# Retention and a routed layer of experts on one core: the decay spread by a matmul, sends ahead of expert 0's cut, 224 columns in expert 0's halves

## The chip, the core and the metric

One core of a Trainium2 chip runs the whole program. The time is the device time of one execution in microseconds (us), the median of the runs shown. Engines: TensorE (PE; its weight loads are PEld), VectorE (DVE), ScalarE (ACT), GpSimd (POOL) and SyncE (SP), which issues most DMAs. Each engine works through its instructions in the order of the program; the order is written out by hand.

## What is computed

q, k and v are (4, 8, 768, 64): batch, heads, positions, head size. A linear attention with a decay per head gives x, 3072 tokens of 512 features, and each token goes through the one expert of eight that its gate chooses:

```python
state = gamma[None, :, None, None] * state + np.einsum('bhd,bhe->bhde', k[:, :, t], v[:, :, t])
y[:, :, t] = scale * np.einsum('bhd,bhde->bhe', q[:, :, t], state)
...
logits = x @ w_gate
expert_idx = np.argmax(logits, axis=1)
...
h = np.maximum(xe @ w1[e], 0.0)
ye = h @ w2[e]
out[mask] = gate_w[mask, None] * ye
```

w1 is (8, 512, 1024), w2 is (8, 1024, 512), all in float32.

## The kernel before

The 3072 tokens are 24 chunks of 128, six to a batch. A loop (L442) takes them in 12 pairs, a = 2k and b = 2k+1. In a pair `scores` multiplies k and q (TensorE) and VectorE multiplies the result by the masks M (L242), `carry` and `output` add the state's part and the chunk's part into Y, `turn_out` multiplies Y by the decay G into xT (VectorE, L288), and `update` adds the chunk into the state, from `vs`, which is v scaled by GpSimd in `scale` (L228). `gate_rows` belongs to the pair before: `logits`, then `rows` (transposes on TensorE into `xp`, copied by ScalarE into the ring `xn`), then `finish_logits`.

When a group of six, four or two chunks has its logits, `gating` chooses the expert (`choose`), takes the exponential (`soft`), counts places with small products (`rank`, `slots`, `advance`) and computes the weights. `send_x` then has GpSimd scatter the 128 rows of a chunk into a table in DRAM, `xs_dram`, by expert (indirect DMA, L629): 24 sends, spread over the pairs by the table SENDS. FETCHES and SPLITS say in which pair expert 0's weights are loaded and split into a high and a low part (L135 on ScalarE, L136 on VectorE or GpSimd). These products take three terms: high by high, high by low and low by high.

Expert 0 is done in two halves of up to EARLY = 256 tokens: those of the first two batches while the attention still runs, the others behind it. After pair 9, `load_x` (L170) and `load_meta` read the first half's rows back from DRAM. In the last pair VectorE turns them (`turn_slices`, L639), ScalarE casts the high part and GpSimd subtracts for the low part (`cut_slices`, L648 and L649, tile xhl). `hidden` (L671) and `result` (L688) are expert 0's two layers for this half; `fill(n)` puts n half steps of `hidden` between the last steps of the gate. The second half (`xg1`, `xhl1`) and the experts 1 to 7 follow in `moe_main` (L818, L843, L845).

The loads of q, k and v go into a ring of five buffers, so load(2k+5) waits until pair k has used its own. SP issues all of them, the weights, `load_x` and the zeroing of rows behind a region, in the order of the program. GpSimd takes its `scale`, its splits, the sends and the low parts in the order of the program too.

Of the kernel before, what the change touches and what calls it, by code (L numbers as in the profile page):

```python
# [20 lines left out]
P = 128  # L21
# [6 lines left out]
CAPS = [256, 452, 424, 412, 400, 392, 376, 360]  # L28
EARLY = 256
# [28 lines left out]
for _name, _w in (("causal", 128), ("cv", 6 * H), ("ratio", 6 * (H // 2)), ("ident", 128), ("iota", 128),  # L58
                  ("desc", 16), ("tok", NTOK), ("blk", 24), ("ebase", E9),
                  ("rev", E1), ("eid", E1), ("caps", E1), ("row", 4), ("slot", JMAX), ("place", 4)):  # L60
    OFF[_name] = (_n, _n + _w)
    _n += _w
# [4 lines left out]
def _constants():  # L67
# [3 lines left out]
    def put(name, v):  # L71
# [6 lines left out]
    put("iota", np.broadcast_to(p[None, :].astype(np.float64), (P, P)))  # L78
# [16 lines left out]
    g = np.repeat(turned[:, :, None] ** (np.arange(C) + 1.0)[None, None, :] / np.sqrt(np.float64(D)), D, axis=0)  # L95
    u = (p[:, None] < p[None, :]).astype(np.float64)
    return (c.astype(np.float32), np.ascontiguousarray(g.astype(np.float32)),
            u.astype(np.float32))
# [3 lines left out]
def retention_moe(ctx, tc, qkv, wg, wts, cst, gdec, ustr, out):  # L102
# [86 lines left out]
    with ExitStack() as actx:  # L189
# [138 lines left out]
        def gating(k):  # L328
# [29 lines left out]
            def rank():  # L358
                pf = v["pf"] = ps_s.tile([P, NB, E9], F32, name="pf", tag="sp")
# [47 lines left out]
        us32 = rawp.tile([P, P], F32, name="us32", tag="raw")  # L407
# [17 lines left out]
        nc.sync.dma_start(out=us32, in_=ustr)  # L425
# [10 lines left out]
        def gate_rows(k):  # L436
            logits(k - 1)
            rows(2 * k - 2)
            rows(2 * k - 1)
            finish_logits(k - 1)  # L440

        for k in range(NCH // 2):  # L442
# [13 lines left out]
            carry(b, c == 0)  # L456
            sends = list(range(*SENDS.get(k, (0, 0))))
# [24 lines left out]
            output(a)  # L482
# [3 lines left out]
            if not last:  # L486
                update(b + 1)
            if k == 1:
                nc.vector.tensor_copy(out=us, in_=us32)
                nc.vector.tensor_scalar(out=run, in0=k_("ebase"), scalar1=1.0 / P, scalar2=None, op0=ALU.mult)  # L490
                nc.vector.tensor_copy(out=wgs[:, :, E:E + 1], in_=wgs[:, :, 0:1])
                gate_rows(k)
            for g in range(2 * k + AHEAD, min(2 * k + AHEAD + 2, NCH)):
                load(g, slice(0, 4 if g % CPB < CPB - 1 else 3))
            if k == 1:
                for e in (0, E):
                    clear(slice(e * N + FILLED, e * N + FILLED + ZROWS))
            if k == 9:
# [4 lines left out]
            if k in FETCHES:  # L503
                fetch(0, FETCHES[k])

        stages["rank"]()
        for name in ("slots", "advance", "weights"):
            stages[name]()
        for g in range(SENDS[NCH // 2 - 1][1], GROUPS[-2][0]):
            send_x(g)  # L510
# [3 lines left out]
        rows(NCH - 1)  # L514
        for g in range(GROUPS[-2][0], GROUPS[-1][0]):
            send_x(g)
        fill(FILL[1])
        finish_logits(NCH // 2 - 1)
        final = gating(len(GROUPS) - 1)
        final["choose"]()  # L520
        final["soft"]()
        for i in (12, 13):
            split(0, *divmod(i, 4), nc.vector, 1)
        fill(FILL[2])
        lows(2, nc.gpsimd)
        final["rank"]()
        final["slots"]()
        final["weights"]()
        for i in (14, 15):
            split(0, *divmod(i, 4), nc.vector, 1)  # L530
        for g in range(GROUPS[-1][0], NCH):
            send_x(g)
# [13 lines left out]
        with nc.allow_low_precision(reason="one nonzero term, a small integer"):  # L546
            nc.vector.tensor_reduce(out=eid7, in_=se, axis=AX.X, op=ALU.add)

# [38 lines left out]
        pieces = ((0, P), (4, P // 2), (6, P // 2))  # L587
# [69 lines left out]
def early_half(tc, yo, rx, wp, ps, wparts, xhl, sidx0, meta0, out):  # L657
# [6 lines left out]
    def hidden(f, part=None):  # L664
# [16 lines left out]
    def result(j, part):  # L681
        if part == 0:
            pys[j] = ps.tile([P, DM], F32, name="py0", tag="sp")
        py = pys[j]
        for f in range(4 * part, 4 * part + 4):
            whi, wlo = wparts[0, 2 + f // 4]
            for i, (a, h) in enumerate(((whi, hh), (wlo, hh), (whi, hl))):
                nc.tensor.matmul(out=py, lhsT=h[:, f, j * P:(j + 1) * P], rhs=a[:, f % 4, :],  # L688
# [3 lines left out]
        nc.vector.tensor_scalar(out=sliced(yo[:, j, :]), in0=featured(py), scalar1=meta0[:, j, 1:2], scalar2=None,  # L692
                                op0=ALU.mult)

    def send(j):
        scatter_rows(tc, out, sidx0[:, j:j + 1], yo[:, j, :])
# [5 lines left out]
def moe_main(ctx, tc, wparts, fetch, split, xhl1, xgs, clear_behind, load_x, load_meta, token_index, regions, beyond, limit, natural,  # L702
# [14 lines left out]
    pys = [ps_y.tile([P, DM], F32, name=f"py{i}") for i in range(2)]  # L717
    out_slices = out.rearrange("n (q m) -> (n q) m", q=4)
# [56 lines left out]
    with tc.manual_schedule():  # L775
        for e in range(E):
# [222 lines left out]
```

## Time and profile before

| | |
|---|---|
| median of 3 runs | 404.08 us (403.95 to 404.31) |
| the profiled execution | 404.0 us |
| its span, first to last instruction | 402.2 us |
| TensorE busy | 388.8 us, 97% |
| VectorE, ScalarE, GpSimd busy | 249.9, 154.0, 165.8 us |
| DMA | 80.55 MB, mean 200 GB/s |

Times in the views are microseconds from the first instruction. The timeline gives for each group of neighbouring instructions its start, its length, engine, line, operation, result and operands, and in brackets the idle time of the engine before it with what ended the idle time. Neighbouring products overlap, so a group's length is not the sum of its products. The attention takes the first 100 us, expert 0's first half about 100 to 125, its second half 125 to 148, the other experts the rest.

### The profile page before, as it was taken

How to read it: one execution, taken by the hardware profiler on the slowest of the kernel's cores; microseconds unless marked ns; L12 is line 12 of the kernel's file. 1: busy time of each engine (PE TensorE's matmuls, PEld its weight loads, DVE VectorE, ACT ScalarE, POOL GpSimd, SP SyncE). 2: the span in 40 equal slices, each digit the busy share in tenths (PEclk: the TensorE clock that was granted, in tenths of full speed). 3: DMA queues.
4: the chain of work that ended last, by engine and by line, in shares of the span. 5: the costliest groups of instructions: out<-in, count | busy, mean ns of one | idle time of the engine just before them, and what ended most of it. 6: DMA issues, size and time to landing. Idle time of an engine off the chain costs nothing. (4 is left out here: it accounts for less than half of the span.)

```text
span 402.2 us, 8329 instructions
## 1 busy us (share of the span) xinstructions
PE 388.8 (97%) x3276; PEld 359.4 (89%) x3276; DVE 249.9 (62%) x467; ACT 154.0 (38%) x307; POOL 165.8 (41%) x152
## 2 busy tenths in 40 slices
PE   8889999998999999999999999999999999999994
PEld 4778888896989979999999999999999999999972
DVE  4448757786685577672866387467738657675410
ACT  2236345463623444431543245145324515523200
POOL 0334536854771032000386057118605822850741
PEclk9999999999999999999999999999999999999999
DMA  7998799982547959365348347915654783530111
GB/s 278 404 417 304 264 406 424 404 363 76 213 135 208 255 175 285 115 175 143 123 146 228 115 137 235 233 51 210 203 145 130 246 216 107 165 128 2 53 47 48
DMA packets 30745, 80.55 MB, mean 200 GB/s; under 512 B 5130, under 2 KB 19342, under 8 KB 24176
## 3 DMA queue, kind: packets, MB, share of 16 engines
q1 hardware_dynamic: 25664, 67.31, 51.6%
q0 software_dynamic: 5040, 12.69, 8.4%
q8 instruction: 26, 0.43, 0.4%
q14 instruction: 15, 0.12, 0.1%
HBM read 65.50 MB, written 15.22 MB: 201 GB/s over the span
## 5 line engine op out<-in xcount | busy, mean ns | idle before, releaser
L629 POOL DMA_INDIRECT out<-Z,sidx x80 | 94.0, 1176 | 136.9 <-DVE Z L770 115.6
L136 DVE TENSOR_TENSOR wlo<-raw,whi 128x1024 fp32r<-128x1024 f32 (+1 forms) x66 | 79.1, 1200 | 16.6 <-ACT whi L135 16.2
L135 ACT CAST whi<-raw 128x1024 fp32r<-128x1024 f32 (+1 forms) x72 | 67.4, 951 | 5.0 <-DMA raw<-w 5.0
L823 ACT ACTIVATE hh<-ph 128x256 fp32r<-128x256 f32 (+7 forms) x64 | 31.5, 492 | 93.1 <-PE ph L818 92.8
L845 PE MATMUL py<-hh,whi 128*128 128x452 f32 (+5 forms) x192 | 66.9, 349 | 0.0
L845 PE MATMUL py<-hl,whi 128*128 128x452 f32 (+5 forms) x192 | 66.8, 348 | 0.0
L845 PE MATMUL py<-hh,wlo 128*128 128x452 f32 (+5 forms) x192 | 66.8, 348 | 0.0
L824 DVE SCALAR_TENSOR_TENSOR hl<-ph,hh 128x256 fp32r<-128x256 f32 (+7 forms) x64 | 35.5, 555 | 34.4 <-ACT hh L823 33.7
L818 PE MATMUL ph<-xh,whi 128*128 128x452 f32 (+6 forms) x224 | 50.1, 345 | 0.5 <-ACT xh L648 0.5
L818 PE MATMUL ph<-xl,whi 128*128 128x452 f32 (+6 forms) x224 | 50.2, 345 | 0.0
L818 PE MATMUL ph<-xh,wlo 128*128 128x452 f32 (+6 forms) x224 | 50.0, 345 | 0.0
L818 PEld LDWEIGHTS ph<-xh,whi 128*128 128x128 f32 x224 | 40.6, 188 | 1.6 <-ACT xh L648 0.9
L818 PEld LDWEIGHTS ph<-xl,whi 128*128 128x128 f32 x224 | 40.8, 188 | 0.7
L818 PEld LDWEIGHTS ph<-xh,wlo 128*128 128x128 f32 x224 | 40.7, 188 | 0.7
L648 ACT CAST xh<-xt 128x512 fp32r<-128x512 f32 (+7 forms) x26 | 14.3, 554 | 60.8 <-DVE xt L639 60.8
L845 PEld LDWEIGHTS py<-hl,whi 128*128 128x128 f32 x192 | 36.0, 188 | 0.8
L845 PEld LDWEIGHTS py<-hh,whi 128*128 128x128 f32 x192 | 36.1, 188 | 0.7
L845 PEld LDWEIGHTS py<-hh,wlo 128*128 128x128 f32 x192 | 36.1, 188 | 0.7
L228 POOL TENSOR_TENSOR vs<-qkv_t,cs 128x512 f32<-128x512 f32 x19 | 20.1, 1059 | 35.5 <-DMA qkv_t<-qkv 32.9
L242 DVE TENSOR_TENSOR Sb<-sp,xgs 128x512 f32<-128x512 f32 x48 | 29.9, 682 | 4.9 <-PE sp L239 4.9
L765 DVE STREAM_TRANSPOSE Z<-py 128x416 f32<-128x416 f32 (+3 forms) x24 | 15.0, 627 | 27.3 <-PE py L845 27.2
L629 POOL DMA_INDIRECT xs_dram<-xn,KEY x24 | 24.6, 1026 | 17.4 <-DVE xt L639 7.7
(130 smaller groups left out, 528.8 us busy)
## 6 DMA issues: line engine op xcount, KB each, us to landing
raw<-w SPq DMA_DIRECT2D x32, 1024.0 KB, 5.6
qkv_t<-qkv SPq DMA_DIRECT2D x19, 1024.0 KB, 9.6
qkv_t<-qkv SPq DMA_DIRECT2D x4, 768.0 KB, 7.7
xgs<-xs_dram SPq DMA_DIRECT2D x12, 211.2 KB, 4.7
xgs<-xs_dram SPq DMA_DIRECT2D x8, 195.0 KB, 4.0
out<-Z,sidx POOLq DMA_INDIRECT x80, 4.0
xs_dram<-zero SPq DMA_DIRECT2D x6, 195.0 KB, 5.7
qkv_t<-qkv SPq DMA_DIRECT2D x2, 512.0 KB, 7.0
```

Of the source, the lines that this page charges most:

```text
L135: nc.scalar.copy(out=hi[:, h], in_=raw[:, h])
L136: engine.tensor_tensor(out=lo[:, h], in0=raw[:, h], in1=hi[:, h].bitcast(F32), op=ALU.subtract)
L228: engine.tensor_tensor(out=vs, in0=qs[g][:, 2].rearrange("a (h d) -> a h d", d=D), in1=cv[:, c, :].unsqueeze(2).broadcast_to([P, H, D]), o ...
L242: nc.vector.tensor_tensor(out=Sb[:, r], in0=sps[r], in1=M[:, r], op=ALU.mult)
L629: sc = tc.nc.gpsimd.indirect_dma_start(out=out, out_offset=bass.IndirectOffsetOnAxis(ap=index, axis=0), in_=rows, in_offset=None, bounds_c ...
L648: nc.scalar.copy(out=xh[:, :, sl], in_=src)
L765: nc.vector.transpose(out=Zs[e][:, 0:nb, k, :], in_=py[:, 0:32 * nb].rearrange("p (j c) -> p j c", c=32))
L818: nc.tensor.matmul(out=ph[:, :cap], lhsT=wparts[e, f // 4][a][:, kd, fo:fo + P], rhs=x[:, kd, :cap], start=(n == 0), stop=(n == 3 * KD - 1))
L823: nc.scalar.activation(out=hh[:, :cap], in_=ph[:, :cap], func=AF.Relu)
L824: nc.vector.scalar_tensor_tensor(out=hl[:, :cap], in0=ph[:, :cap], scalar=0.0, in1=hh[:, :cap].bitcast(F32), op0=ALU.max, op1=ALU.subtract)
L845: nc.tensor.matmul(out=py[:, :cap], lhsT=a[:, f % 4, k * P:(k + 1) * P], rhs=x[:, :cap], **se)
```

## The change

- G is no longer loaded (256 KB). A table of 2 x 640 numbers is, ahead of the first q, k and v; one product spreads it over 128 partitions into PSUM and ScalarE copies it to G. Four of 13 warm products go. The strictly lower triangle `us` is computed from two tables instead of loaded, and `iota` has 8 columns instead of 128. Chunks 0 and 1 change buffers in the ring.
- In the first pair `output(a)` stands ahead of `update(b)`; in the second `gate_rows(1)` ahead of `update(b + 1)`.
- `rank`, `slots`, `advance` and `weights` of a whole batch stand at the end of the pair in which `choose` was made, not in the next.
- Pairs 10 and 11 send chunks 12 to 17 (three each) instead of 12 to 15; those of the last pair stand ahead of its `gate_rows`. Chunks 16 and 17 had followed the loop. The fetch of expert 0's last quarter of weights moves from pair 8 to pair 9, ahead of `load_x`.
- In the last pair `turn_slices` stands behind the masks, and `cut_slices` between the logits and the `rows`.
- EARLY and CAPS[0] are 224 instead of 256. `hidden` takes its terms in the order high by high, low weights by high x, high weights by low x, six products to a half step. The last `rank` follows after 4 half steps instead of 8, the first two low parts of `hidden` are VectorE's, and two splits follow later.
- In expert 0's second half the four preparations of expert 1's x stand together ahead of the two splits that stood between them.

```diff
-CAPS = [256, 452, 424, 412, 400, 392, 376, 360]
-EARLY = 256
+CAPS = [224, 452, 424, 412, 400, 392, 376, 360]
+EARLY = 224
...
-WARM = 13
-FILL = (2, 2, 4, 2)
+WARM = 9
+FILL = (2, 2, 2, 2)
...
+HALVES = ((0, P), (P // 32, EARLY - P))
...
-SENDS = {4: (0, 1), 5: (1, 3), 6: (3, 5), 7: (5, 7), 8: (7, 10), 9: (10, 12), 10: (12, 13), 11: (13, 16)}
+SENDS = {4: (0, 1), 5: (1, 3), 6: (3, 5), 7: (5, 7), 8: (7, 10), 9: (10, 12), 10: (12, 15), 11: (15, 18)}
...
-FETCHES = {1: 0, 4: 1, 6: 2, 8: 3}
+FETCHES = {1: 0, 4: 1, 6: 2, 9: 3}
...
+        qs[1], qs[0] = [ld.tile([P, 4, DM], F32, name="qkv_t", tag="ld") for _ in range(2)]
         nc.sync.dma_start(out=cs[:, 0:NFIRST], in_=cst[:, 0:NFIRST])
+        nc.sync.dma_start(out=g2, in_=gdec)
         load(0)
         load(1, slice(0, 2))
-        nc.sync.dma_start(out=G, in_=gdec)
         load(1, slice(2, 4))
...
+        spread = ps_m.tile([P, NP, C], F32, name="spread", tag="mm")
+        nc.tensor.matmul(out=spread, lhsT=g2[:, DM:], rhs=g2[:, 0:DM], start=True, stop=True)
+        nc.scalar.copy(out=G, in_=spread)
...
         def gate_rows(k):
             logits(k - 1)
+            if k == NCH // 2 - 1:
+                for j, w in HALVES:
+                    cut_slices(nc, nc.gpsimd, xhl[:, 0], xhl[:, 1], xt0, j, w)
             rows(2 * k - 2)
...
-            if last:
-                xt0 = ld.tile([P, KD, EARLY], F32, name="xt0", tag="ld")
-                for j in (0, 4):
-                    turn_slices(nc, xt0, xg0, j, P)
-                for j in (0, 4):
-                    cut_slices(nc, nc.gpsimd, xhl[:, 0], xhl[:, 1], xt0, j, P)
             if k:
                 scores(a)
             scores(b)
             carry(a, True)
             carry(b, c == 0)
+            if last:
+                xt0 = ld.tile([P, KD, EARLY], F32, name="xt0", tag="ld")
+                for j, w in HALVES:
+                    turn_slices(nc, xt0, xg0, j, w)
...
+            if last:
+                for i in sends:
+                    send_x(i)
+                sends = []
             if k > 1:
                 gate_rows(k)
-                if batch > 0 and c == 2:
-                    for name in ("rank", "slots", "advance", "weights"):
-                        stages[name]()
+            if k == 0:
+                output(a)
             if c < CPB - 2:
                 update(b)
...
-            if not last:
-                update(b + 1)
             if k == 1:
-                nc.vector.tensor_copy(out=us, in_=us32)
+                nc.vector.tensor_tensor(out=us, in0=causal, in1=ident, op=ALU.subtract)
...
                 gate_rows(k)
+            if not last:
+                update(b + 1)
+            if batch > 0 and c == 0:
+                stages["rank"](ps_m, "mm")
+                for name in ("slots", "advance", "weights"):
+                    stages[name]()
...
-        for kd in (range(KD) if part is None else range(2 * part, 2 * part + 2)):
-            for i, (a, x) in enumerate(((whi, 0), (whi, 1), (wlo, 0))):
-                nc.tensor.matmul(out=phs[f], lhsT=a[:, kd, fo:fo + P], rhs=xhl[:, x, kd, :],
-                                 start=(kd == 0 and i == 0), stop=(kd == KD - 1 and i == 2))
+        order = [(a, x, kd) for a, x in ((whi, 0), (wlo, 0), (whi, 1)) for kd in range(KD)]
+        for i, (a, x, kd) in list(enumerate(order))[6 * part:6 * part + 6]:
+            nc.tensor.matmul(out=phs[f], lhsT=a[:, kd, fo:fo + P], rhs=xhl[:, x, kd, :],
+                             start=(i == 0), stop=(i == len(order) - 1))
...
-                    if not e and j in (1, 3):
-                        split(1, 2, *halves[j // 2])
+                if not e and k == 0:
+                    for i, eng in halves:
+                        split(1, 2, i, eng)
```

## Rows read from the trace of the kernel before

**Rows 1.** The profile page: busy time by engine, and the DMA engines in 40 slices.
```profile
PE 388.8 (97%) x3276; PEld 359.4 (89%) x3276; DVE 249.9 (62%) x467; ACT 154.0 (38%) x307; POOL 165.8 (41%) x152
...
DMA  7998799982547959365348347915654783530111
```

**Rows 2.** The waits of TensorE: us in total, times, longest us.
```profile
PE U L253 <- POOL vs L228: 2.9, 2, 1.5
PE xp L295 <- DVE Sb L242: 1.7, 1, 1.7
PE sp L239 <- DMA qkv_t<-qkv: 1.1, 3, 0.4
PE ph L818 <- ACT xh L648: 0.5, 1, 0.5
PE py L843 <- DVE hl L824: 0.2, 1, 0.2
```

**Rows 3.** The timeline, first 25 us: G's load and the waits of the first pairs.
```profile
2.15 0.43 SPq L412 DMA_DIRECT2D xgs<-gdec  x1
...
12.76 1.04 POOL L228 TENSOR_TENSOR vs<-qkv_t,cs 128x512 f32<-128x512 f32 x1 [1.37 <-DMA qkv_t<-qkv]
...
19.97 1.29 DVE L288 TENSOR_TENSOR xT<-Y,xgs 128x512 f32<-128x512 f32 x2 [1.82 <-PE Y L280]
...
21.42 0.69 PE L253 MATMUL U<-vs,qkv_t 128*64 128x64 f32 x16 [1.50 <-POOL vs L228]
21.45 0.16 DVE L491 COPY xgs<-xgs 128x4 f32<-128x4 f32 x1
```

**Rows 4.** The timeline from 81 to 102 us: sends, expert 0's x, the first hidden products.
```profile
81.87 1.03 POOL L629 DMA_INDIRECT xs_dram<-xn,KEY  x1 [0.16 <-issue]
...
89.10 2.97 SPq L170 DMA_DIRECT2D xn<-xs_dram  x4
...
94.64 1.30 DVE L639 STREAM_TRANSPOSE xt<-xn 128x512 f32<-128x512 f32 x2 [2.47 <-DMA xn<-xs_dram]
...
95.53 1.01 POOL L629 DMA_INDIRECT xs_dram<-xn,KEY  x1 [7.74 <-DVE xt L639]
...
96.57 2.53 POOL L649 TENSOR_TENSOR xhl<-xt,xhl 128x512 fp32r<-128x512 f32 x2
...
96.57 1.25 PE L295 MATMUL xp<-cs,xT 128*128 128x128 f32 x8 [1.69 <-DVE Sb L242]
...
100.02 0.48 PE L671 MATMUL ph<-xhl,whi 128*128 128x256 f32 x2
...
100.56 0.98 POOL L629 DMA_INDIRECT xs_dram<-xn,KEY  x1 [0.30 <-issue]
...
101.62 0.64 PE L310 MATMUL L<-xT,xgs 128*32 128x256 f32 x8
```

**Rows 5.** Windows: length, busy us (count) of PE, PEld, DVE, ACT, POOL, clock, DMA share, GB/s.
```profile
44.00:46.00 2.00, 2.00 (x48) 2.00 (x44) 1.07 (x6) 0.92 (x4) 0.81 (x1) 1.00 0.36 49
...
80.00:88.00 8.00, 8.00 (x151) 7.06 (x150) 7.02 (x15) 4.88 (x15) 6.08 (x6) 1.00 1.01 421
```

**Rows 6.** The second half's start in the timeline; then groups by form (busy us, mean ns).
```profile
125.08 0.64 PE L818 MATMUL ph<-xhl,whi 128*128 128x256 f32 x4
...
L818 PE MATMUL ph<-xh,wlo 128*128 128x452 f32 x32 | 7.8, 365 | 0.0
...
L818 PE MATMUL ph<-xhl,wlo 128*128 128x256 f32 x32 | 5.1, 283 | 0.0
```

**Rows 7.** The timeline's warm products at the start, and windows around the end of TensorE's work.
```profile
1.08 4.62 PE L420 MATMUL warm<-ones 128*128 128x512 bf16 x13 [1.08 <-DVE ones L146]
...
4.46 0.75 PEld L420 LDWEIGHTS <-ones 128*128 128x128 bf16 x4 [0.27 <-issue]
...
395.00:400.00 5.00, 1.25 (x6) 0.58 (x4) 0.48 (x1) 0.47 (x1) 1.01 (x1) 1.00 0.14 36
400.00:402.20 2.20, 0.00 (x0) 0.00 (x0) 0.00 (x0) 0.00 (x0) 0.00 (x0) 0.59 0.03 13
```

More of the change, by code (lines that the diff above doesn't have):

```diff
@@ L43 @@
 ZROWS = 96
-WARM = 13
-FILL = (2, 2, 4, 2)
+WARM = 9
+FILL = (2, 2, 2, 2)
 AHEAD = 5
 BIG = 1 << 20
+HALVES = ((0, P), (P // 32, EARLY - P))
 GROUPS = ((0, 6), (6, 6), (12, 6), (18, 4), (22, 2))
-SENDS = {4: (0, 1), 5: (1, 3), 6: (3, 5), 7: (5, 7), 8: (7, 10), 9: (10, 12), 10: (12, 13), 11: (13, 16)}
+SENDS = {4: (0, 1), 5: (1, 3), 6: (3, 5), 7: (5, 7), 8: (7, 10), 9: (10, 12), 10: (12, 15), 11: (15, 18)}
 SPLITS = {3: (0, 1), 4: (2, 3), 7: (4, 5), 8: (6, 7), 9: (8, 9), 10: (10, 11)}
-FETCHES = {1: 0, 4: 1, 6: 2, 8: 3}
+FETCHES = {1: 0, 4: 1, 6: 2, 9: 3}
 OFF = {}
 _n = 0
-for _name, _w in (("causal", 128), ("cv", 6 * H), ("ratio", 6 * (H // 2)), ("ident", 128), ("iota", 128),
+for _name, _w in (("causal", 128), ("cv", 6 * H), ("ratio", 6 * (H // 2)), ("ident", 128), ("iota", 8),
                   ("desc", 16), ("tok", NTOK), ("blk", 24), ("ebase", E9),
@@ L77, in _constants @@
     put("causal", (p[None, :] >= p[:, None]).astype(np.float64))
-    put("iota", np.broadcast_to(p[None, :].astype(np.float64), (P, P)))
+    put("iota", np.broadcast_to(np.arange(8)[None, :], (P, 8)))
     pos = (np.arange(6)[None, :] * C + p[:, None] + 1).astype(np.float64)
@@ L94, in _constants, with retention_moe @@
     turned = gamma.reshape(2, 2, 2).transpose(1, 2, 0).reshape(2, NP)
[L95 to L98, printed above, removed]
+    g = np.zeros((2, DM + P), np.float64)
+    g[:, 0:DM] = (turned[:, :, None] ** (np.arange(C) + 1.0)[None, None, :] / np.sqrt(np.float64(D))).reshape(2, DM)
+    g[:, DM:] = np.repeat(np.eye(2), D, axis=1)
+    return c.astype(np.float32), g.astype(np.float32)
 @with_exitstack
-def retention_moe(ctx, tc, qkv, wg, wts, cst, gdec, ustr, out):
+def retention_moe(ctx, tc, qkv, wg, wts, cst, gdec, out):
     nc = tc.nc
@@ L356, in soft, with rank @@
                 nc.scalar.activation(out=ex, in_=sh, func=AF.Exp)
-            def rank():
-                pf = v["pf"] = ps_s.tile([P, NB, E9], F32, name="pf", tag="sp")
+            def rank(space, tag):
+                pf = v["pf"] = space.tile([P, NB, E9], F32, name="pf", tag=tag)
                 nc.tensor.matmul(out=pf[:, 0:n, :], lhsT=us, rhs=Eb, start=True, stop=False, skip_group_check=True)
@@ L405, in lows @@
             state["low"] = n
-        us32 = rawp.tile([P, P], F32, name="us32", tag="raw")
+        g2 = rawp.tile([2, DM + P], F32, name="g2", tag="raw")
         vs0 = ld.tile([P, H, D], F32, name="vs0", tag="ld")
+        qs[1], qs[0] = [ld.tile([P, 4, DM], F32, name="qkv_t", tag="ld") for _ in range(2)]
         nc.sync.dma_start(out=cs[:, 0:NFIRST], in_=cst[:, 0:NFIRST])
+        nc.sync.dma_start(out=g2, in_=gdec)
         load(0)
         load(1, slice(0, 2))
-        nc.sync.dma_start(out=G, in_=gdec)
         load(1, slice(2, 4))
@@ L424, in retention_moe @@
         nc.sync.dma_start(out=wgs[:, :, 0:E], in_=wg.rearrange("(k p) e -> p k e", p=P))
-        nc.sync.dma_start(out=us32, in_=ustr)
         for r in range(2):
@@ L481, in retention_moe @@
                 stages["soft"]()
-            output(a)
+            if k:
+                output(a)
             output(b)
@@ L497, in retention_moe @@
                     clear(slice(e * N + FILLED, e * N + FILLED + ZROWS))
+            if k in FETCHES:
+                fetch(0, FETCHES[k])
             if k == 9:
@@ L502, in retention_moe @@
                 load_meta(meta0, 0, 2)
-            if k in FETCHES:
-                fetch(0, FETCHES[k])
-        stages["rank"]()
+        stages["rank"](ps_s, "sp")
         for name in ("slots", "advance", "weights"):
             stages[name]()
-        for g in range(SENDS[NCH // 2 - 1][1], GROUPS[-2][0]):
-            send_x(g)
         fill(FILL[0])
@@ L514, in retention_moe @@
         rows(NCH - 1)
+        finish_logits(NCH // 2 - 1)
         for g in range(GROUPS[-2][0], GROUPS[-1][0]):
@@ L517, in retention_moe @@
         fill(FILL[1])
-        finish_logits(NCH // 2 - 1)
         final = gating(len(GROUPS) - 1)
@@ L521, in retention_moe @@
         final["soft"]()
+        lows(2, nc.vector)
+        final["rank"](ps_s, "sp")
+        fill(FILL[2])
+        final["slots"]()
+        final["weights"]()
+        for g in range(GROUPS[-1][0], NCH):
+            send_x(g)
         for i in (12, 13):
             split(0, *divmod(i, 4), nc.vector, 1)
[L524 to L532, printed above, removed]
         fill(FILL[3])
@@ L547, in retention_moe @@
             nc.vector.tensor_reduce(out=eid7, in_=se, axis=AX.X, op=ALU.add)
+        for i in (14, 15):
+            split(0, *divmod(i, 4), nc.vector, 1)
         past = gsm.tile([P, E1], F32, name="past")
@@ L586, in retention_moe @@
         xhl1 = new_xhl()
-        pieces = ((0, P), (4, P // 2), (6, P // 2))
+        pieces = ((0, P), (4, 64), (6, EARLY - P - 64))
         for j, w in pieces:
@@ L662, in early_half, with hidden @@
     phs, pys = {}, {}
-    def hidden(f, part=None):
+    def hidden(f, part):
         whi, wlo = wparts[0, f // 4]
@@ L683, in result @@
             pys[j] = ps.tile([P, DM], F32, name="py0", tag="sp")
-        py = pys[j]
+        py, w = pys[j], min(P, EARLY - j * P)
         for f in range(4 * part, 4 * part + 4):
@@ L687, in result @@
             for i, (a, h) in enumerate(((whi, hh), (wlo, hh), (whi, hl))):
-                nc.tensor.matmul(out=py, lhsT=h[:, f, j * P:(j + 1) * P], rhs=a[:, f % 4, :],
+                nc.tensor.matmul(out=py[:w], lhsT=h[:, f, j * P:j * P + w], rhs=a[:, f % 4, :],
                                  start=(f == 0 and i == 0), stop=(f == KF - 1 and i == 2))
@@ L691, in result @@
             return
-        nc.vector.tensor_scalar(out=sliced(yo[:, j, :]), in0=featured(py), scalar1=meta0[:, j, 1:2], scalar2=None,
+        nc.vector.tensor_scalar(out=sliced(yo[:w, j, :]), in0=featured(py[:w]), scalar1=meta0[:w, j, 1:2], scalar2=None,
                                 op0=ALU.mult)
     def send(j):
-        scatter_rows(tc, out, sidx0[:, j:j + 1], yo[:, j, :])
+        w = min(P, EARLY - j * P)
+        scatter_rows(tc, out, sidx0[:w, j:j + 1], yo[:w, j, :])
     return hidden, low, result, send
@@ L717, in moe_main @@
     pys = [ps_y.tile([P, DM], F32, name=f"py{i}") for i in range(2)]
+    nc.vector.memset(pys[1][widths[0][1]:, CAPS[1]:], 0.0)
     out_slices = out.rearrange("n (q m) -> (n q) m", q=4)
```

4 lines of the change are left out of this document (2 added, 2 removed).

## Prediction

> **What bounds the kernel now.** I read the busy shares first: TensorE is busy for 97% of the span [rows 1], so a change pays only where it takes work from TensorE or closes one of its gaps. The waits of TensorE come next [rows 2]. They are few: 2.9 us for the scaled v of the first pairs (`vs` before `update`), 1.7 us at the transposes of `rows`, 1.1 us for loads of q, k and v, and 0.5 and 0.2 us around expert 1's start. The rest of the span is products back to back, so what is saved in a dense stretch moves the end by as much, unless something else is late there. I then read the timeline around each gap.
>
> The 1.7 us gap is the clearest. In the last pair VectorE starts with the transposes of expert 0's x and waits for them until 94.64; the masks (L242) queue behind, and the transposes on TensorE, which need the masks' PSUM buffers, start at 96.57 after 1.69 us of idleness [rows 4]. The DMA engines are the second limit: they are full or nearly so from 10 to 30 us and from 50 to 90 [rows 1], but only 0.36 busy from 44 to 46 [rows 5].
>
> **The start.** G as a 5 KB table instead of 256 KB, no table for `us` and fewer columns of `iota` take some 0.38 MB out of a full queue, 0.9 us at 0.42 MB/us. But the small table is issued ahead of load(0), and one issue costs SP 0.43 us (G's own [rows 3]), so the first data come that much later. The two-instruction spread product takes the place of the last of the four warm products that are dropped; G's copy is on an idle ScalarE. I count both at nothing (0 to 0.5 us if they were in the way). `output(0)` moves into the first wait for `vs`, 1.4 us of the 2.9 [rows 2]; that closes this wait, but the next one takes over: `update(2)` needs the third chunk's `vs`, which GpSimd starts at 12.76, after a wait for its load, and ends at 13.80 [rows 3]. What is gained is only what the loads come sooner, 0.1 to 0.5 us. In the second pair `gate_rows(1)` goes ahead of `update(4)`, which waits 1.50 us until 21.42 [rows 3]. It can't use that time: its first product reads `wgs`, whose last column VectorE writes at 21.45 (L491), behind the products with G that start at 19.97 [rows 3]. The two orders then end together. So the start gives 0.1 us (0 to 0.6).
>
> **The middle.** Ranks move from the second to the first pair after `choose`: the same seven small products and eight VectorE operations, now ahead of the next masks. The masks come some 1.5 us later, still ahead of the `rows` that need their buffers; TensorE loses nothing (0 to 0.4 us each, three times). The first send may go about 3 us sooner, into the slack at 44 to 46 [rows 5]; loads after that come up to 1 us earlier, and the wait of 0.4 us for a load, the longest of the three [rows 2], which lies at 62 us, should go. All this is absorbed by what follows.
>
> **The last pair, where it is decided.** With the masks ahead of expert 0's x, the 1.69 us gap closes, and TensorE reaches the first hidden product at about 97.9 instead of 100.02 (less 1.7 and 0.4). Eight products on, at 98.7 (twelve take 1.6 us until 101.62 [rows 4], less with fewer columns), it needs the low part `xl` of x. That is GpSimd's `cut_slices`, and there the order on GpSimd turns. Before, one send (12) stood ahead of it: send at 95.53, cut at 96.57, ready at 99.10. After, sends 12 to 17 stand ahead. The first of them can't go before expert 0's x has been read out of the same DRAM rows: the reads are issued at 89.10, after send 11 (issued 81.87) has landed, and the send follows at 95.53 [rows 4]. (The name given there for its releaser comes after it in the program, so it was the reads.) From that start S, five more sends follow at 1.28 us each (0.98 and 0.30 idle), the cut 1.04 after the last, and its two parts take 1.27 and, at 96 columns, 0.95: `xl` is ready at S + 9.7.
>
> S itself: the 1 MB fetch now follows load(23) instead of standing ahead of send 11's landing. It cost up to 2.5 us there (1.05 MB at 0.42 MB/us [rows 5]); but load(23) and the same fetch are still in the queue when send 11 goes, since that waits for `vs` and a split behind load(20). I take half, 1.3 us, with 0 and 2.6 as bounds: S = 94.2 (92.9 to 95.5), `xl` at 103.9. TensorE waits 5.2 us, at a place where nothing later can pass it.
>
> From there the sum is: four products, then what now lies between 101.62 (the last logits) and 125.08 (expert 0's second half), 23.5 us without a gap [rows 4, 6]. The products of 256 columns become 224. A product's duration is 365 ns at 452 columns and 283 ns at 256, 0.42 ns a column [rows 6], so 32 columns are 13.4 ns: 84 products give 1.1 us back. `rank` now follows the logits after 12 products instead of 36, so it may wait 0.15 us for `choose`. The second half starts at xl + 0.4 + 23.5 - 1.1 + 0.15 = xl + 22.9. Then 96 products more, 1.3 us, and the 0.7 us around expert 1's start: its x is now prepared ahead of the splits, and TensorE comes later anyway. Against now: xl + 22.9 - 125.1 - 1.3 - 0.7 = xl - 104.2, or S - 94.5. With S = 94.2 the change is worth -0.3 us (-1.6 to +1.0). After that TensorE is dense to the end and passes it on. The chain of sends to the reads for the second half ends sooner too (all sends follow S without the stop that `low` made), so it doesn't take over. `result(1)` with 96 rows in place of 128 still streams 512 columns and saves nothing.
>
> On the columns: at 256 columns the weights' load and the stream can't be told apart in these rows, as no narrower product of this kind is in the trace. The Trainium skill, "TensorE: Matmul & The Clock Gate", section "LDWEIGHTS (loading the stationary operand)", puts a load at columns divided by 1.2 ns, 107 ns for 128 columns, which is also what 256 columns take at 2.4 GHz. By that rule 224 columns would save nothing, and the sum would be +2.1 us.
>
> **The profiled execution** took 404.0 us, 1.8 more than its span, and the median is 404.08. So the forecast is 403.7 us, from 402.4 to 405.0 by its own bounds. About 0.2% (0.8 us) is what a measurement can tell from no change.
>
> **Rivals.**
> 1. *GpSimd is in time.* If S is 89 or less, because send 11 lands 6 us sooner with an emptier queue, TensorE doesn't wait: -5.5 us, 398.5; halfway (S = 91.5) -3 us, 401. For it: the fetch is gone from ahead of the send, and sends start sooner. Against it: the engines are full from 48 to 88, and no bytes are removed there. 0.27, for 398.5 to 402.4.
> 2. *The long wait costs the clock* (slower). After the last product near 396.25 the granted clock is still 1.00 up to 400, then falls to the lower level, 1.2 GHz, with a mean of 0.59 in the last 2.2 us: some 4.1 us after the last product [rows 7]. A wait for `xl` of 5.2 us could do the same, from xl = 102.8 on. Of the thirteen warm products at the start nine lie in the 3.4 us before 4.46, and the weights of the last four are loaded in 0.75 us, 0.2 apart [rows 7]: nine would take 1.8 us at that pace, so such a stretch costs 1.6. With the late `xl` that makes +1.3 us, 405.3 (404.9 to 406.9). One fall is all that the trace shows, so I don't make it the forecast. 0.24.
> 3. *224 columns give nothing*, by the load of the weights or otherwise: +2.1 us, 406.1. No row shows fewer than 256 columns in this number format. 0.12.
> 4. *224 columns are dearer.* A plain f32 product of 128 columns takes two instructions, 1.25 us for four [rows 4], 2.4 ns a column; at that rate 192 products of 224 columns would cost about 80 us more. Only the lack of a row speaks for it. 0.05.
>
> The forecast itself has 0.32.
>
> **How the numbers follow.** Faster by over 0.2% (under 403.2): the first rival and 0.4 of the forecast, 0.40. Within 0.2%: 0.4 of the forecast and a fifth of the second rival, 0.18. Slower: the rest, 0.42. The range leaves out the dear columns and the far end of the first rival: 399.6 to 406.9.
>
> **What would show it.** In the changed kernel's timeline: TensorE's idle time before the hidden products that read `xl`, put down to GpSimd, and its length; the start of send 12 (94.2 here); the granted clock just after; the duration of a product of 224 columns (270 ns here); VectorE's copy into `wgs` as the releaser of the first logits, near 21.5; and no wait of the last `rows` for masks. The forecast is wrong if send 12 starts before 92.9, if `xl` doesn't wait for six sends, or if the products' durations don't go by columns.

## The result, and the profile after

The changed kernel takes 408.75 us in the median of four runs. One of the four, at 775 us, was disturbed; here and below, medians are of all executions, while ratios leave disturbed ones out. The others are 407.26, 407.82 and 409.69. Against the kernel before (404.01) their ratio is 1.0107, 95% interval 1.0065 to 1.0149: slower, by about 4 us, where the forecast was 403.7 and its range ended at 406.9. The profiled execution took 407.26 us with a span of 405.4, 3.2 more than before.

The busy time of the changed kernel, from its page, beside [rows 1]:

```profile
PE 390.5 (96%) x3274; PEld 360.2 (89%) x3274; DVE 245.6 (61%) x470; ACT 154.2 (38%) x308; POOL 163.0 (40%) x150
```

TensorE has two instructions fewer and 32 columns fewer in 192 products, and yet is busy 1.7 us longer. That can't be a wait, as waits aren't busy; something made the same products longer. The waits of TensorE answer [rows 2]:

```profile
PE ph L683 <- POOL xhl L661: 5.3, 1, 5.3
PE L L311 <- DVE xgs L499: 1.7, 1, 1.7
PE warm L423 <- DVE ones L147: 1.1, 1, 1.1
PE sp L240 <- DMA qkv_t<-qkv: 0.5, 1, 0.5
```

The two waits for `vs` (2.9 us) and the wait for the masks (1.7) are gone; one for GpSimd's low part of x, 5.3 us, and one for VectorE's copy into `wgs`, 1.7 us, have come. The timeline from 88 to 106 us answers [rows 4]:

```profile
89.38 2.49 SPq L171 DMA_DIRECT2D xn<-xs_dram  x4
...
94.91 1.01 POOL L641 DMA_INDIRECT xs_dram<-xn,KEY  x1 [6.60 <-DVE Sb L243]
...
98.23 0.68 PE L683 MATMUL ph<-xhl,whi 128*128 128x224 f32 x4
98.75 0.61 PE L683 MATMUL ph<-xhl,wlo 128*128 128x224 f32 x4
...
101.35 0.97 POOL L641 DMA_INDIRECT xs_dram<-xn,KEY  x1 [0.30 <-issue]
102.33 2.23 POOL L661 TENSOR_TENSOR xhl<-xt,xhl 128x512 fp32r<-128x512 f32 x2
104.61 1.19 PE L683 MATMUL ph<-xhl,whi 128*128 128x224 f32 x4 [5.26 <-POOL xhl L661]
```

Send 12 starts at 94.91, five more follow, the cut (L661) starts behind them, and TensorE stands from 99.36 to 104.61. Four products of one form take 0.68 us ahead of the wait and 1.19 behind it. The windows show why (length, then busy us and count of PE, PEld, DVE, ACT, POOL, granted clock, DMA share, GB/s):

```profile
98.20:104.60 6.40, 1.16 (x13) 0.97 (x11) 2.43 (x10) 0.00 (x0) 5.43 (x6) 0.90 0.48 185
104.60:110.20 5.60, 5.59 (x29) 4.58 (x29) 0.88 (x5) 2.29 (x5) 3.93 (x4) 0.50 0.38 149
110.20:130.25 20.05, 20.05 (x132) 17.27 (x132) 13.53 (x45) 8.18 (x22) 6.93 (x8) 1.00 0.45 144
```

The granted clock is 0.90 in the mean of the wait, and then 0.50, the level of 1.2 GHz, for 5.6 us in which TensorE never stands. In the kernel before, the windows up to 400 us read 1.00 ([rows 5] and [rows 7] show some of them). The start of expert 0's second half in the timeline answers [rows 6]:

```profile
130.25 0.60 PE L832 MATMUL ph<-xhl,whi 128*128 128x224 f32 x4
```

And the group by form (busy us, mean ns), for the 283 ns of 256 columns there:

```profile
L832 PE MATMUL ph<-xhl,wlo 128*128 128x224 f32 x32 | 4.9, 274 | 0.0
```

The second half starts 5.17 us later than before (125.08); from there to the end 2.0 us are won back.

### The profile page after: what moved, and what is told of

The parts are those of the page before. It is cut to its first block, busy times and chain, and to the rows that moved or that the text cites. A ratio compares the mean times of both kernels' runs of the same rounds, so it can differ in the third digit from the quotient of the medians.

```text
span 405.4 us, 8329 instructions
## 1 busy us (share of the span) xinstructions
PE 390.5 (96%) x3274; PEld 360.2 (89%) x3274; DVE 245.6 (61%) x470; ACT 154.2 (38%) x308; POOL 163.0 (40%) x150
## 4 chain that ended last, share of the span: by engine, by line
PE 68%; issue 3%; POOL 2%; DVE 0%; POOLq 0%; ACT 0%; ACTq 0%
PE ph L832 32%; PE py L860 26%; PE ph L683 3%; PE py L700 3%; PE py L858 3%; POOL out L641 2%; PE xp L296 0%; PE L L311 0%; DVE hl L838 0%; POOLq L627 0%; ACT hh L837 0%; PE lp L321 0%; DVE Z L784 0%; POOLq L641 0%; PE pf L365 0%
## 5 line engine op out<-in xcount | busy, mean ns | idle before, releaser
L137 DVE TENSOR_TENSOR wlo<-raw,whi 128x1024 fp32r<-128x1024 f32 (+1 forms) x66 | 76.6, 1165 | 11.4 <-ACT whi L136 10.7
L837 ACT ACTIVATE hh<-ph 128x224 fp32r<-128x224 f32 (+7 forms) x64 | 31.3, 489 | 97.3 <-PE ph L832 97.1
L838 DVE SCALAR_TENSOR_TENSOR hl<-ph,hh 128x224 fp32r<-128x224 f32 (+7 forms) x64 | 35.3, 552 | 36.4 <-ACT hh L837 35.7
```

The source lines that it names most:

```text
L137: engine.tensor_tensor(out=lo[:, h], in0=raw[:, h], in1=hi[:, h].bitcast(F32), op=ALU.subtract)
L837: nc.scalar.activation(out=hh[:, :cap], in_=ph[:, :cap], func=AF.Relu)
L838: nc.vector.scalar_tensor_tensor(out=hl[:, :cap], in0=ph[:, :cap], scalar=0.0, in1=hh[:, :cap].bitcast(F32), op0=ALU.max, op1=ALU.subtract)
```

## The experiments

Each kernel ran in a series on one chip with the kernel before beside it, and is compared with that one. This matters: before took 404 us in the series of e1 to e4 and in that of u1, but 411 to 412 us in those of s and c, of r, of t and of u2. What differs there stands under t1.

### e1: the cut behind three sends instead of six

```diff
-            if k not in (4, 10) and sends:
+            if k not in (4, 10, 11) and sends:
...
-            if last:
-                for i in sends:
-                    send_x(i)
-                sends = []
```

Expected of e1:

> The changed kernel, with the cut of expert 0's x on GpSimd behind sends 12 to 14 alone; 15 to 17 follow it. Theory A (the low part waits for the sends that stand ahead of it on GpSimd, 1.28 us each): three sends less, so the low part is ready near 100.7 instead of 104.6, TensorE waits about 1.4 us instead of 5.3, the granted clock doesn't fall, and the time is near 401.5 us. Rival B (the wait is for the rows read back from DRAM, whatever stands on GpSimd): the wait stays above 4 us and the time near 407. Rival C (the later sends are now late and hold up the second half): TensorE waits 1.4 us, but again before expert 0's second half, and the time is 403 or more.

Measured: 403.64 us (402.09 to 408.11), before 404.41, ratio 1.0001 (0.997 to 1.0033). The wait for the low part is gone and the second half starts at 125.35. So the wait, with the clock behind it, is what made the changed kernel slow: without it the time is that of the kernel before. It isn't the 401.5 of theory A, though, and rival C's second wait, ahead of the second half, isn't there. Another wait has come, for the operand of the ranks. e1's waits of TensorE:

```profile
PE pf L361 <- DVE EA L351: 2.3, 1, 2.3
```

and its timeline from 97 to 102 us:

```profile
98.16 2.93 DVE L351 TENSOR_TENSOR EA<-eq,ed 128x32 bf16<-128x32 f32 x1
...
98.81 2.22 POOL L657 TENSOR_TENSOR xhl<-xt,xhl 128x512 fp32r<-128x512 f32 x2
...
101.14 0.18 PE L361 MATMUL pf<-EA,us 128*128 128x36 bf16 x1 [2.27 <-DVE EA L351]
```

A VectorE operation on 32 columns, 0.19 us in the changed kernel, took 2.93 us and ended at 101.09, 0.06 us behind the end of GpSimd's subtraction (101.03). Moved away from the sends, the cut met VectorE. (By the profile the operation started 0.65 us ahead of the subtraction; why it didn't end before that isn't shown.)

### e2: the cut behind one send

```diff
-SENDS = {4: (0, 1), 5: (1, 3), 6: (3, 5), 7: (5, 7), 8: (7, 10), 9: (10, 12), 10: (12, 15), 11: (15, 18)}
+SENDS = {4: (0, 1), 5: (1, 3), 6: (3, 5), 7: (5, 7), 8: (7, 10), 9: (10, 12), 10: (12, 13), 11: (13, 18)}
```

together with the edit of e1.

Expected of e2:

> The changed kernel, with only send 12 ahead of the cut, as before the change; 13 to 17 follow the cut. Theory A: the low part is ready near 98.2, TensorE doesn't wait, the clock holds, expert 0's second half starts near 122.3 (125.1 before the change, 130.2 after), and the time is near 399.7 us. Rival B (the read from DRAM): a wait stays and the time is 404 or more. Rival C (the later sends become the bound): TensorE waits before expert 0's second half for its x, and the time lies between 401 and 404.

Measured: 403.97 us (402.26 to 405.73), ratio 0.9989 (0.9969 to 1.001), where theory A had 399.7. The time lies in rival C's range, but TensorE doesn't wait ahead of the second half (125.67). The same meeting as in e1 shows three operations earlier, in e2's timeline:

```profile
98.43 2.23 POOL L657 TENSOR_TENSOR xhl<-xt,xhl 128x512 fp32r<-128x512 f32 x2
98.44 2.28 DVE L345 TENSOR_TENSOR eq<-lg,mx 128x32 f32<-128x32 f32 x1
...
101.44 0.18 PE L361 MATMUL pf<-EA,us 128*128 128x36 bf16 x1 [1.62 <-DVE EA L351]
```

VectorE's operation ends at 100.72 and GpSimd's at 100.66. It stands wherever the cut stands, so it is the cut that holds VectorE up, not the choice. A later run, t2, has it at a third place, an addition on 9 columns that takes 0.17 us in the changed kernel:

```profile
103.91 2.23 POOL L654 TENSOR_TENSOR xhl<-xt,xhl 128x512 fp32r<-128x512 f32 x2
104.17 2.00 DVE L382 TENSOR_TENSOR run<-run,tot 128x9 bf16<-128x9 bf16 x1
```

The Trainium skill, "SBUF — State Buffer", section "SBUF: two separate sides", says that VectorE operations with two SBUF inputs and GpSimd operations that read SBUF take one shared pair of ports by an exclusive lock, for a whole instruction. The ends agree with that, 0.04 to 0.06 us behind GpSimd's in the three; but GpSimd's x2 is two instructions, and VectorE waited through both.

### e3: the wait filled with products

```diff
-        fill(FILL[0])
+        fill(1)
+        idle = ps_m.tile([P, 512], F32, name="idle", tag="mm")
+        for i in range(48):
+            w = 128 if i < 24 else 192
+            nc.tensor.matmul(out=idle[:, 0:w], lhsT=wparts[0, 0][0][:, i % 4, 0:P], rhs=xhl[:, 0, i % 4, 0:w],
+                             start=True, stop=True)
+        fill(FILL[0] - 1)
```

Expected of e3:

> The changed kernel with 48 products that nothing reads, of the three-term kind, 24 of 128 columns and 24 of 192, put between the first and the second half step of the hidden layer, where TensorE waits. The wait for the low part stays (it is ready near 104.6). Theory D (the long wait lets the clock fall, and that costs 2.7 us on top of the wait): the granted clock stays at 1.00 from 98 to 112 and the time is near 404.6 us. Without D: 407 or more. On columns: if a product's cost went by its columns alone (0.42 ns each), 128 columns would stand 0.067 us apart and 192 columns 0.093; if the load of the weights sets a floor, both stand 0.11 apart, as 224 columns do now.

Measured: 407.16 us (406.18 to 408.49), ratio 1.0063 (1.0034 to 1.0092). By its total that is the forecast without D (407 or more), so the total doesn't show the clock's price; the trace does. e3's timeline:

```profile
100.95 5.51 PE L527 MATMUL idle<-xhl,whi 128*128 128x128 f32 x48
...
107.47 0.70 PE L689 MATMUL ph<-xhl,whi 128*128 128x224 f32 x4 [0.77 <-POOL xhl L667]
```

and its windows, with the columns as above:

```profile
107.47:112.00 4.53, 4.51 (x43) 3.90 (x44) 1.48 (x8) 2.70 (x7) 3.50 (x4) 1.00 0.37 145
112.00:130.67 18.67, 18.67 (x118) 15.95 (x117) 13.07 (x41) 7.57 (x21) 6.52 (x9) 1.00 0.58 179
```

Here the clock holds 1.00 and TensorE gets 43 products into 4.53 us, where the changed kernel got 29 into 5.60. From the first product that reads the low part to the second half it takes 130.67 - 107.47 = 23.20 us; in the changed kernel the same work takes 130.25 - 104.61 = 25.64. The half clock costs 2.4 us. e1 and e2, which don't wait for the low part and hold 1.00, confirm the work's time at the full clock; e1's timeline:

```profile
102.24 0.61 PE L679 MATMUL ph<-xhl,whi 128*128 128x224 f32 x4
...
125.35 0.60 PE L828 MATMUL ph<-xhl,whi 128*128 128x224 f32 x4
```

That is 23.11 us, and 23.13 in e2. e3's total gained less, since in this execution the last pair's scores came 2.0 us later (93.34 against 91.36), and send 12 with them (97.75 against 94.91).

### e4: 256 columns in the changed kernel

`CAPS[0]` and `EARLY` back at 256.

Expected of e4:

> The changed kernel with 256 columns in expert 0's halves instead of 224. The 13.4 ns a product of the prediction: 180 products behind the wait cost 2.4 us more, and the low part comes 0.3 later, so 2.7 us over the changed kernel. The 8.3 ns that the changed kernel's trace shows: 1.5 and 0.3, 1.8 us over it, near 409.3 against 407.5.

Measured: 410.02 us (409.68 to 410.52), ratio 1.0142 (1.0118 to 1.0166): 2.2 us above the changed kernel's 407.82, between the two forecasts, so the total doesn't decide. The wait is longer, as the cut is and as its sends came later (send 12 at 96.87; e4's waits of TensorE):

```profile
PE ph L683 <- POOL xhl L661: 6.7, 1, 6.7
```

From the first to the last of the 96 products of the second half it takes 11.39 us, 0.120 each; in the changed kernel 10.60, 0.112 each. So a product gained 8.4 ns by 32 columns, and 192 of them 1.6 us. The clock was back sooner here: it reads 0.50 from the first product behind the wait (106.83) to 110, and 1.00 from 111 on. From there to the second half it takes 132.03 - 106.83 = 25.20 us; with 23.2 at the full clock and 0.7 for the wider columns of 84 products, the half clock cost about 1.3 us, not 2.4. Its price isn't one number.

### c1 and r4: the 224 columns alone, in the kernel before

Expected of c1:

> The kernel before with only the 224 columns in expert 0's halves. By the spacing seen in the changed kernel (0.112 us at 224 columns, 0.120 at 256) 192 products give 1.6 us, of which those ahead of expert 1 that TensorE doesn't wait behind: 402.4 to 403.4. By the forecast's 13.4 ns a product 2.6 us: 401.5. By a floor at 128 rows' load, nothing: 404.

Expected of r4:

> The kernel before with only the 224 columns in expert 0's halves. By 8.3 ns a product (0.112 us at 224 columns, 0.120 at 256, from the changed kernel and its twin with 256) 192 products give 1.6 us: 402.4 to 403.2. By the forecast's 13.4 ns, 2.6 us: 401.5. By a floor at the load of 128 columns of weights: 404.

Measured: c1 412.93 us, ratio 1.0002 (0.9955 to 1.005); r4 411.37, ratio 0.9994 (0.994 to 1.0049), before 412.1 and 411.85. The intervals are as wide as the effect, so the totals decide nothing. The trace does: 95 steps of the second half in 10.60 us, 0.112 each, as in the changed kernel.

### s1, r1, t2, u1: the changed kernel with the old start

G as a 256 KB load, 13 warm products, the old order of the first two pairs; the rest as changed.

Expected of s1:

> The changed kernel with the start of the kernel before (G loaded as 256 KB, 13 warm products, the old order of the first two pairs); the middle, the last pair and the 224 columns are as changed. Theory A (the loss is TensorE's wait for the low part of x and the clock behind it; the start is worth about nothing): the same wait, 5.0 to 5.5 us near 99, the clock at 0.5 for 6.8 us behind it, and 406.5 to 408. Theory B (the start costs 1 to 2 us in most executions, by loads that land later and a clock that rises late): pair 11's scores at 91.2 or sooner, and 405 to 406.5.

Expected of r1:

> The changed kernel with the start of the kernel before, once more on another chip, since on the last one VectorE and ScalarE stood for 3 to 5 us with nothing to wait for in the profile (before itself took 412 us there). Theory A (wait for the low part and the clock behind it): wait 5.0 to 5.5 us, 0.5 for 6.8 us, 406.5 to 408. Theory B (the new start costs 1 to 2 us in most executions): 405 to 406.5, with less spread than the changed kernel.

Expected of t2:

> The changed kernel with the start of the kernel before. If the start costs nothing: equal to t1 within 0.5 us. If it costs 1 to 2 us in most executions: 1 to 2 us below t1. The wait for the low part stays, 5.0 to 6.0 us, and the clock falls behind it for 6.8 us.

Expected of u1:

> The changed kernel with the start of the kernel before. If before takes 404 here: 407.0 to 407.6 if the start costs the 0.4 us that pair 11's scores show, 407.8 if it costs nothing, 406 if it costs 2. If before takes 412 here, the same as t2: 410 to 413, and nothing about the start.

Measured, with before at 404.66: u1 408.0 us (406.86 to 408.91), ratio 1.0097 (1.0074 to 1.0121), against 1.0107 for the changed kernel. (With before at 412, s1, r1 and t2 took 410.23, 411.64 and 413.32 us: 0.9938 (0.989 to 0.9986), 0.9969 (0.9917 to 1.0021) and 0.9998 (0.9957 to 1.0038).) The start makes no difference to the total that these intervals, 0.2 to 0.5% to either side, can tell. The wait and the half clock are there again, in u1's waits of TensorE:

```profile
PE ph L676 <- POOL xhl L654: 5.1, 1, 5.1
```

and in its windows:

```profile
98.00:104.25 6.25, 1.13 (x13) 0.94 (x10) 2.40 (x10) 0.00 (x0) 5.29 (x6) 0.92 0.47 180
104.25:110.03 5.78, 5.78 (x29) 4.77 (x30) 1.03 (x7) 2.29 (x5) 3.92 (x4) 0.50 0.40 158
```

That is the second trace for the clock's price: 129.97 - 104.25 = 25.72 us, again 2.5 more than e3.

The start isn't free for all that. The third pair's scores begin at 25.1 us in the mean of the six profiles with the new start (24.30 to 25.97) and at 23.9 in the fourteen with the old one (23.65 to 24.35); at the last pair 92.4 and 91.8 are left. The profiled changed kernel has hardly any of it left there, 91.36 against 91.22 before. Nor does the wait for the low part swallow it where it is left, as send 12 comes later too: at 94.56 with the last pair at 91.13 (u1), 94.91 with 91.36 (changed), 95.24 and 96.87 with 92.08 (e1, e4), 97.39 with 93.02 (e2) and 97.75 with 93.34 (e3). In e1 and e2 the last pair starts at 92.08 and 93.02, which is one reason why they are no faster than before.

### s3, r3, t3: the old start and the filled wait

Expected of s3:

> The first of these three with 48 products that nothing reads (24 of 128 and 24 of 192 columns, some 5.3 us) in the wait for the low part. Clock theory: the clock stays at 1.00, the 5.3 us are filled, under 1 us of wait is left, and the time is 2 to 3 us below the first of the three. Rival (the half clock costs little, because what follows waits for something else anyway): equal to the first within 0.7 us.

Expected of r3:

> The first of these with 48 unread products in the wait for the low part. Clock theory: the clock stays at 1.00 from 5 to 390 us, under 1 us of wait is left, and the time is 2 to 3 us below the first. Rival (the half clock costs little): equal to the first within 0.7 us.

Expected of t3:

> t2 with 48 unread products in the wait. If the half clock costs what the changed kernel's trace shows (2.8 us more from the low part to the second half): 2 to 2.8 us below t2, less 0 to 0.8 for what the 48 products are longer or shorter than the wait. If the clock costs little: equal to t2.

Measured: 412.12, 414.11 and 414.87 us, ratios 1.001, 1.0022 and 1.0063 (before 411.9 to 412.1). Each is 1.5 to 2.5 us above the unfilled kernel of its series (410.23, 411.64 and 413.32), where 2 to 3 us below was forecast. They were meant to give the clock's price without the new start, and didn't: in these executions TensorE stood among the 48 products themselves, 1.6 to 2.2 us with no releaser, the clock fell all the same, and the products ended behind the low part (in t3 it was ready at 107.20, and TensorE came to it at 110.1). The price rests on e1, e2 and e3 against the changed kernel and u1.

### t1: the changed kernel beside them

Expected of t1:

> The changed kernel itself, as the mark for the next three on the same chip. 407 to 408.5 if before is at 404, with a spread of 2 us or more by the start's clock and loads.

Measured: 411.81 us (410.98 to 414.65), before 411.99, ratio 0.9994 (0.996 to 1.0028). In this series the change cost nothing that the interval shows. t1's timeline shows what was different:

```profile
98.63 0.19 DVE L355 TENSOR_TENSOR sh<-lg,mx 128x32 f32<-128x32 f32 x1
...
102.68 1.29 DVE L289 TENSOR_TENSOR xT<-Y,xgs 128x512 f32<-128x512 f32 x2 [3.87 <-remote]
...
106.64 0.77 PE L683 MATMUL ph<-xhl,whi 128*128 128x224 f32 x2 [6.22 <-POOL xhl L661]
```

VectorE stands 3.87 us ahead of L289, though the product that it waits for is done. In the changed kernel this lies inside TensorE's wait for the low part. In the timeline of r4, which has the order of before, it meets TensorE itself:

```profile
109.02 0.37 ACT L312 COPY xgs<-L 128x256 f32<-128x256 f32 x1 [2.09 <-remote]
109.44 0.69 PE L320 MATMUL lp<-cs,xgs 128*128 128x128 f32 x2 [4.69 <-issue]
...
112.06 0.23 DVE L325 TENSOR_REDUCE lg<-lp 128x16 f32<-128x64 f32 x1 [9.16 <-remote]
```

There the order of before loses about what the changed one loses by its wait. This reading rests on r4; the kernel before itself left no profile in these series.

### s2, r2, t4, u2: no cut on GpSimd

The old start, ScalarE's cast as before, and the subtraction on VectorE right behind the choice of pair 10; GpSimd keeps only the sends, the last three of them behind `gate_rows`:

```diff
...
                 stages["choose"]()
+                if last:
+                    for j, w in HALVES:
+                        sl = slice(32 * j, 32 * j + w)
+                        nc.vector.tensor_tensor(out=xhl[:, 1, :, sl], in0=xt0[:, :, sl],
+                                                in1=xhl[:, 0, :, sl].bitcast(F32), op=ALU.subtract)
                 stages["soft"]()
...
```

Expected of s2:

> The same with no cut on GpSimd at all: ScalarE casts as before, VectorE subtracts right behind the choice of pair 10 (two operations), GpSimd has the sends alone. Theory (wait, clock and the collision of VectorE with GpSimd's subtraction are what the change lost): no wait for the low part over 0.5 us, VectorE's operation at the choice back at 0.2 us where it took 2.9, the rank's wait gone or under 0.7 us, second half at 122 to 123.5 and 399.5 to 401.5. Rival (the sends themselves hold VectorE up, or a later wait takes over): the choice's operations stay over 1 us or expert 1 starts after 147, and 402.5 to 404.

Expected of r2:

> The same with the subtraction on VectorE right behind the choice of pair 10, GpSimd with the sends alone. Theory: no wait for the low part over 0.5 us, the clock held, the choice's operations at 0.2 us each (they were in the last run, 97.14 to 98.0), second half at 122 to 123.5, 399.5 to 401.5. Rival (the xT product, which waits behind the subtraction, takes over): a wait of over 1 us at the last logits, 402 to 404.

Expected of t4:

> t2 with the subtraction on VectorE, right behind the choice of pair 10: no wait for the low part over 0.5 us and the clock held. Wait and clock together: 7 to 8 us below t2, 399.5 to 401.5 if before is at 404. If VectorE's later xT product holds the last logits up: a wait over 1 us there, and 402 to 404.

Expected of u2:

> Old start, subtraction on VectorE right behind the choice of pair 10, GpSimd with the sends alone. If before takes 404 here and no engine stands still without a cause: no wait for the low part, the clock held, second half at 122 to 123.5, 399.5 to 401.5. If the last logits wait over 1 us for the xT product behind the subtraction: 402 to 404.

Measured: 410.97, 411.29, 410.24 and 410.39 us, all with before at 411.2 to 412.1; ratios 0.9953 (0.9904 to 1.0001), 0.9903 (0.9863 to 0.9943), 0.9957 (0.9927 to 0.9988), 0.996 (0.9927 to 0.9993). By the ratios it is 0.4 to 1% faster than before, though s2's interval reaches 1 and the medians differ by 0.1 to 0.4% only; in t4 it is 1.6 us below the changed kernel of the same series. Against the old start with the cut on GpSimd, in the same series, the medians are 0.7 us higher (s2), 0.4 lower (r2) and 3.1 lower (t4): that it gains anything there isn't shown. u2's timeline:

```profile
97.73 0.19 DVE L351 TENSOR_TENSOR EA<-eq,ed 128x32 bf16<-128x32 f32 x1
97.84 1.15 DVE L484 TENSOR_TENSOR xhl<-xt,xhl 128x512 fp32r<-128x512 f32 x2
...
99.47 0.61 PE L678 MATMUL ph<-xhl,whi 128*128 128x224 f32 x4
101.99 1.29 DVE L289 TENSOR_TENSOR xT<-Y,xgs 128x512 f32<-128x512 f32 x2 [2.87 <-remote]
103.42 0.64 PE L311 MATMUL L<-xT,xgs 128*32 128x256 f32 x8 [3.34 <-remote]
```

L351 is back at 0.19 us, the low part is there at 98.99, and TensorE doesn't wait for it. With no other GpSimd work than sends, these operations are not held up, so e1's stretch was the cut's. What comes next is VectorE standing ahead of L289 again, and that costs TensorE 3.3 us here, with the granted clock at 0.68 in the mean from 103.4 to 106 us and at 0.78 from there to 110. The 399.5 to 401.5 us that I expected with before at 404 were never measured: none of the four met such a series.

## Why the prediction was wrong, and where it was right

Right were the views and the place. TensorE's gap for the masks closed; the first hidden product came at 98.23 (97.9 forecast); the order on GpSimd decided; the wait for the low part was 5.26 us (5.2); `wgs` took over the start, with VectorE's copy at 21.66 and the logits at 21.88 (21.5).

Wrong was the step that carries the time from the low part to the second half, put at xl + 22.9. It measured 25.7 (xl 104.56, second half 130.25), and that is 2.8 of the 3.6 us by which the profiled execution (407.26) missed 403.7:

- *The clock was held in the sum.* That is the failed step. The text had the mechanism as its second rival, with the point from which it decides (xl over 102.8, and xl was 104.56), and gave it 0.24, because one fall in [rows 7] seemed thin. It fell: the gap is 5.26 us, and [rows 7] had the clock fall 4.1 us after the last product. A row that shows the fall once, after a shorter gap than the one that the sum itself forecasts, should have stood in the sum. Its price was 1.6 us by the warm products and measured 2.4 (e3 against the changed kernel). The rival's own bounds were wrong too: for `xl` from 102.8 to 105.2 its sum gives 404.2 to 406.6, not 404.9 to 406.9.
- *The columns.* 13.4 ns a product was taken from durations of 256 to 452 columns; spacing gives 8.4. Over the 84 products that is the other 0.4 us. The 48 products of e3, at 128 and 192 columns, stand 0.111 us apart (100.95 to the next product at 106.30), as those of 224 do. So for products of this kind there is a floor, which 256 columns pass by 8 ns. The Trainium skill, "TensorE: Matmul & The Clock Gate", section "LDWEIGHTS (loading the stationary operand)", puts a load of weights at its columns divided by 1.2 ns, an estimate of 107 ns for 128 columns, which is near this floor; but that nothing at all would be gained from 256 on, as I read it, was wrong too.
- *S*, the start of send 12: 94.91, not 94.2, inside its bounds, 0.7 us.

Behind the second half the forecast gave 2.0 us back, 1.3 by 96 products and 0.7 at expert 1's start. 2.0 came back, but as 0.8 by the products (10.87 us instead of 11.67) and 1.1 at expert 1.

*The start* was put at +0.1 us gained. It is a loss at the third pair, 1.2 us. `wgs` as the wait that takes over there was named, two things weren't. Where the clock is up, the loads come later, not sooner: GpSimd's `vs` for the fourth chunk, which waits for its load, starts at 16.09 to 16.61 in e1, e3, e4 and t1, and at 15.19 to 15.85 in before, s1, t2 and u1; why, no run shows. And the clock at the start, counted at nothing with four warm products fewer, isn't always up. The window from 8 to 12 us of the changed kernel:

```profile
8.00:12.00 4.00, 4.00 (x54) 3.49 (x52) 2.28 (x4) 0.93 (x4) 1.04 (x1) 0.60 1.03 432
```

the same of e1:

```profile
8.00:12.00 4.00, 3.73 (x80) 3.31 (x78) 2.22 (x4) 1.14 (x5) 1.04 (x1) 1.00 1.03 432
```

and of e2:

```profile
8.00:12.00 4.00, 4.00 (x44) 3.66 (x42) 1.29 (x2) 0.93 (x4) 1.04 (x1) 1.00 1.03 431
```

The changed kernel ran part of this stretch at the half clock (0.60) with 54 products, e1 at the full one with 80. e2 has 44 in a window in which TensorE never stands, although the column reads 1.00; whether its clock was low there isn't shown. So the same start doesn't always go the same way. In the profiled changed kernel 0.1 us of it is left at the last pair (91.36 against 91.22), so it is hardly a cause of that miss.

*The first rival* (GpSimd in time) had 0.27 and needed S at 89 or less; S was 94.91. What took the wait away was not an earlier send but fewer sends ahead of the cut (e1, e2), and even so the gain didn't come, as the account below says.

The account closes: wait 5.3 and clock 2.4 make 7.7 us. e1 takes both away; of that the stretched VectorE operation takes 2.3 back and the start 0.7 (its last pair at 92.08 against 91.36), so 4.7 are left. The second half came 4.9 us sooner, and the totals differ by 4.2 us (403.64 and 407.82).

What stays open: why the clock's price differs between the changed kernel and e4, why VectorE, ScalarE and TensorE stand in some series, and what the version with the subtraction on VectorE gives where before takes 404 us.

## What to carry to other kernels

A wait that a sum forecasts on TensorE is to be priced twice, for its length and for the clock behind it, as soon as any row shows the clock fall after a gap that short. Work that is queued on GpSimd behind others' sends has a second neighbour, VectorE: ask for each place it could go which two-input VectorE operations run beside it and who waits for them. And a loss ahead of a wait for another engine is hidden by it only if that engine's work isn't late for the same reason: t1's wait hid VectorE's standing ahead of L289, but not the late start, as send 12 came later with the last pair.

## What the runs showed of the hardware

- A 32-column VectorE operation took 2.93 us (e1) and 2.28 us (e2) instead of 0.19, a 9-column one 2.00 us (t2) instead of 0.17, each ending 0.04 to 0.06 us behind a pair of GpSimd subtractions.
- The clock fell in a 5.3 us gap and stood at 0.50 for 5.6 us of products without a gap before it rose; 29 products went into that stretch, where 4.53 us at 1.00 took 43. Behind e4's gap of 6.7 us it was back at 1.00 within 4.2 us of products.
- In the series where before takes 412 us, engines stand at the same instruction with nothing to wait for in the profile: VectorE ahead of L289 for 1.9 to 5.1 us in all eleven profiles of changed kernels, TensorE ahead of L320 for 4.69 us in both c1 and r4 (the order of before). In the series at 404 us no such gap of over 1 us shows near there, for the same changed kernel. No run settles the cause.
